# Batches 1 to 3 of a windowed attention: scores by quarters in shared bursts, value products as in batch 0, last stores by quadrant, and a new order

## The chip, the cores and the metric

The kernel runs on one core of a Trainium2 chip. The metric is the device time of one launch in microseconds, the median of several runs. One more execution was recorded by the profiler; all rows shown are from it.

## The reference, cut to what matters

```python
# q, k, v: (4 batches, 8 heads, 768 rows, 64), float32
scores = q @ k.T / 8
keep = (key < 4) | ((0 <= row - key) & (row - key < 128))     # 4 sink keys, a window of 128
a = softmax(where(keep, scores, -1e9))
x = (a @ v), heads side by side                               # (4, 768, 512)
h = relu(x.T @ w_tok1) @ w_tok2                               # mixes the 768 rows
u = x + h.T
out = u + relu(u @ w_ch1) @ w_ch2                             # mixes the 512 channels, 1536 hidden
```

## The kernel before

The work goes by *pairs* of heads: pair p is heads 2·(p mod 4) and the next of batch p div 4, so there are 16 pairs, 0 to 3 in batch 0. One pair's two heads lie on partitions 0 to 63 and 64 to 127, so that products with a contraction of 64 run two at a time on half of the array each (HALVES in the code), four at a time on a quarter each (QUARTERS) and eight at a time (EIGHTHS). Everything else uses the whole array (FULL). Scores are made with keys on partitions. A *group* g (0, 1, 2) of a pair is two blocks of 128 keys with the up to two blocks of 128 queries that see them; `scores(p, g)` writes it to one double bank of PSUM (there are two of these, tag `sc`), ScalarE takes the exponential into `pT`, and VectorE or GpSimd zeroes what lies outside the window. The four sink keys of two pairs are scored together by `score_sinks` (EIGHTHS). The value product multiplies `pT` and `pT_sink` with v, which has a column of ones beside it; VectorE takes the reciprocal of that column's result and scales into `x_sb`.

Batch 0 (`first_attention`) is scored on TensorE with its masks, and its value product is `pv(p, half)`: three query blocks of both heads, with one sink product on the whole array for both heads at a time. Pairs 4 to 15 are made by `attention_and_tokens`, with two bursts for each pair. The first burst holds group 0 in HALVES and the sink part of the value product of the pair before (`sink_values`, also HALVES, one head on each half of the array); `values(p, i)` then adds the window part of one head on the whole array. The second burst holds groups 1 and 2 in QUARTERS and, for even pairs, the sinks' scores:

```python
units.append(burst(scores(p, 0), sink_values(p - 1)))   # with transposed(p + 1) ahead for pairs 5 to 7
units += [values(p - 1, i) for i in range(2)]
units.append(burst(scores(p, 1), scores(p, 2), ...))    # turned_u and score_sinks where they are due
```

q and k arrive with rows on partitions. For pairs 0 to 3 SyncE loads them in float32 and engines cast them; for pairs 4 to 15 GpSimd's queue loads and casts them (two transfers for each of q and k, one for v), in the order written in `LOADS`, eight transfers at a time on the way: `q4` there is q of pair 4, `v` is v, `t` is w_tok, `c` a quarter of w_ch1, `d` a quarter of w_ch2. Pairs 4 to 7 are turned on TensorE (`turn`, `transposed`), pairs 8 to 15 by DMA transposes that SyncE issues (L500); the sinks' columns of kT are then copied to `kTs` by GpSimd or VectorE.

`mix_h` and `mix_u` are the mixing of rows (streams g and h for batch 0, k for the others). `mix_channels` is the mixing of channels: its first half (stream c) is plain for batch 0 and in seven half-size products in place of eight (Strassen's way, in Winograd's form) for batches 1 to 3; its second half, also by sevens, makes x (row blocks 0, 1, 3, 4) and y (2, 5). Each quadrant of a y or x result is added up on VectorE (L1223) into `o_sb`, and SyncE stores it (L1233).

TensorE's order is written out by hand in `ORDERED`, one word for each unit: `a17` is unit 17 of the stream of pairs 4 to 15, `c6` of the channels, and so on. The other engines' order is made by a planner (`Plan`) while the program is built, from written costs and the units' dependencies; at run time each engine takes its instructions in that fixed order and waits on semaphores. `done` maps names like `("qT", p)` to operations, on which others wait. Ahead of a unit stand also the PSUM banks that it needs (tag `mx`, four of them, beside the two double banks).

Of the kernel before, what the change touches and what calls it, by code (L numbers as in the profile page):

```python
# [17 lines left out]
def kernel(  # L18
# [72 lines left out]
    LATER = "cxyak"  # L91
# [380 lines left out]
    def prepare(p):  # L472
# [21 lines left out]
        free = ([("sk", p - 3)] if p >= 3 else [], [("s", p - NKB)] if p >= NKB else [])  # L494
# [109 lines left out]
    def scores(p, g):  # L604
# [4 lines left out]
        quarters = p >= NHP and g > 0  # L609
# [59 lines left out]
        if not by_pe:  # L669
# [8 lines left out]
            (190, 165, 140)[g] if quarters else width(g) * 0.47, run, deps, {} if by_pe else {"sc": [[x]]}, then,  # L678
# [30 lines left out]
    def pv(p, half):  # L709
# [36 lines left out]
        op = unit(460, run, deps, {"mx": [[r, n]]}, [r, n])  # L746
# [228 lines left out]
    def attention_and_tokens():  # L975

        tokens, units = [], []
        first, last = NHP, len(pairs) - 1
        prepare(first)
        units += [turn(first, n) for n in range(2)]  # L980
        for p in range(first, last + 1):
            b, hp = pairs[p]
            pieces = []
            if p < last:
                prepare(p + 1)
                if p + 1 < BY_DMA:
                    pieces.append(transposed(p + 1))
            pieces.append(scores(p, 0))
            if p > first:
                pieces.append(sink_values(p - 1))  # L990
            units.append(burst(*pieces))
            if p > first:
                units += [values(p - 1, i) for i in range(2)]
            pieces = [scores(p, 1), scores(p, 2)]
            if hp == 0 and p > first:
                tokens.append(mix_h(b - 1, 1, 0, NTOK))
                tokens += [mix_u(b - 1, 1, st, 2) for st in range(0, NT, 2)]
                if p <= BY_DMA:
                    pieces.append(turned_u(b - 1, 1))
            if hp == NHP - 1 and p < BY_DMA:  # L1000
                pieces.append(turned_u(b, 0))
            if hp % 2 == 0:
                pieces.append(score_sinks(p + 1))
            units.append(burst(*pieces))
            units[-1].then.append(sink_rows(p))
            if hp == 2:
                tokens.append(mix_h(b, 0, 0, NTOK))
                tokens += [mix_u(b, 0, st, 2) for st in range(0, NT, 2)]
        units += [pv(p, half) for half in range(2)]
        tokens.append(mix_h(b, 1, 0, NTOK))  # L1010
        tokens += [mix_u(b, 1, st, 2) for st in range(0, NT, 2)]
        return units, tokens

    def mix_channels(b):
# [196 lines left out]
        def products(t0, n):  # L1211
# [19 lines left out]
            def store(i):  # L1231
                def run(e):
                    in_order(nc.sync.dma_start(  # L1233
                        out=out[b, (QH * i + t0) * P:(QH * i + t0 + n) * P].rearrange("(t p) c -> p t c", p=P),
                        in_=tiles["o_sb", b, t0][:, i],
# [301 lines left out]
```

## Time and profile before

| | |
|---|---|
| median of three runs | 194.55 us (193.59 to 194.74) |
| profiled execution | 193.02 us, span from first to last instruction 191.3 us |
| TensorE busy | 181.8 us, 95% |
| VectorE, ScalarE, GpSimd busy | 163.7, 107.8, 89.2 us |
| moved by DMA | 26.31 MB, of it 11.80 MB in GpSimd's queue |
| granted TensorE clock | 0.998 of full speed |

In the profile's rows, PE is TensorE's products, PEld its weight loads, DVE is VectorE, ACT is ScalarE, POOL is GpSimd and SP is SyncE, with SPq its DMA issues. A timeline row is the start, the length, the engine, the line, the operation, output and inputs, the shape and how many alike were merged; in brackets stands the idle time ahead of it and what ended it. L157 is the line of the helper by which every matmul is recorded, so that rows are told apart by their tiles: `qT,kT` are scores, `v_sink,pT_sink` the sinks' value products, `v_aug,pT` the window's, `uT,w_ch` and `uT_sums,k_f` the first half of the channels, `w_ch,v1T`, `q_f,v1T` and `q_f,v_sums` the second.

### The profile page before, as it was taken

The page shows a single profiled execution, that of the slowest core. Times are in us where ns is not written, and L with a number is a line of the kernel's source. Part 1 is how long each engine was busy: PE and PEld are TensorE (multiplying, and loading weights), DVE is VectorE, ACT ScalarE, POOL GpSimd, SP SyncE. Part 2 cuts the span into 40 slices and gives each one's busy share as a digit, 9 for nine tenths or more (in the row PEclk, how much of TensorE's full clock was granted, in tenths as well). Part 3 has the DMA queues.
Part 4 walks back from the last instruction along what each step waited for, and adds up shares of the span by engine and source line. Part 5 has one row for each costly group of instructions (what it writes and reads, how often), then busy time and mean ns, then how long its engine had stood idle before and what let it go on. Part 6 is the DMA issues. An engine that isn't in the chain of part 4 may idle for free.

```text
span 191.3 us, 5397 instructions
## 1 busy us (share of the span) xinstructions
PE 181.8 (95%) x2170; PEld 132.5 (69%) x2173; DVE 163.7 (86%) x346; ACT 107.8 (56%) x199; POOL 89.2 (47%) x140
## 2 busy tenths in 40 slices
PE   6889889799999999999999999999999999999992
PEld 1336668466578787866657788876578887658882
DVE  4578848898999998889999999899899987789962
ACT  4499938687976724479785602676861103773000
POOL 7588879879499688453865350140160000000000
PEclk9999999999999999999999999999999999999999
DMA  6999999999999999999999999440102123500035
GB/s 185 251 288 180 178 166 191 186 170 207 173 147 171 113 116 154 181 175 232 186 132 149 137 115 137 167 174 0 33 0 55 29 48 130 211 0 0 0 113 219
DMA packets 92136, 26.31 MB, mean 137 GB/s; under 512 B 82384, under 2 KB 89040, under 8 KB 92112
## 3 DMA queue, kind: packets, MB, share of 16 engines
q0 software_dynamic: 67232, 11.80, 84.7%
q1 hardware_dynamic: 24880, 14.17, 36.5%
q8 instruction: 17, 0.28, 0.6%
q14 instruction: 7, 0.06, 0.1%
HBM read 26.75 MB, written 6.29 MB: 173 GB/s over the span
## 4 chain that ended last, share of the span: by engine, by line
PE 78%; DMA 16%; POOL 3%; issue 1%; SPq 1%; DVE 0%
PE ps L157 77%; DMA k_f<-in_k_dram 7%; DMA w_ch<-in_moe_w_ch_dram 5%; DMA v_aug<-in_v_dram 4%; POOL q_bf L142 1%; SPq L129 1%; POOL v_aug L150 1%; PE ps L542 0%; POOL w_ch L175 0%; POOL k_bf L166 0%; POOL w_tok L175 0%; PE ps L573 0%; DVE o_sb L1223 0%
## 5 line engine op out<-in xcount | busy, mean ns | idle before, releaser
L644 ACT ACTIVATE pT<-ps 128x1024 bf16<-128x1024 f32 (+1 forms) x48 | 44.2, 958 | 20.1 <-PE ps L157 19.8
L164 ACT ACTIVATE parts<-ps 128x384 f32<-128x384 f32 x51 | 23.2, 490 | 20.7 <-PE ps L157 19.3
L157 PE MATMUL ps<-uT,w_ch 128*128 128x384 bf16 x168 | 33.7, 326 | 0.6 <-DMA w_ch<-in_moe_w_ch_dram 0.6
L157 PEld LDWEIGHTS <-v1T 128*128 128x128 bf16 x288 | 28.0, 98 | 4.3
L1111 DVE CUSTOM_DVE_ANT_0 v1T<-ps,parts 128x384 bf16<-128x384 f32 x54 | 28.2, 548 | 2.7 <-PE ps L157 2.3
L157 PEld LDWEIGHTS <-w_ch 128*128 128x128 bf16 x204 | 19.0, 98 | 12.3 <-DMA w_ch<-in_moe_w_ch_dram 1.1
L170 ACT ACTIVATE v1T<-ps 128x384 bf16<-128x384 f32 x40 | 18.6, 498 | 10.2 <-PE ps L157 9.7
L157 PE MATMUL ps<-uT_sums,k_f 128*128 128x384 bf16 x108 | 23.4, 326 | 0.0
L157 PEld LDWEIGHTS <-v_sums 128*128 128x128 bf16 x216 | 20.5, 98 | 3.1 <-issue 0.5
L655 POOL TENSOR_SCALAR_AFFINE_SELECT pT<-pT 128x256 bf16<-128x256 bf16 (+1 forms) x28 | 14.1, 538 | 18.1 <-issue 16.5
L142 POOL DMA_DIRECT2D q_bf<-in_q_dram x24 | 19.7, 828 | 5.0 <-DMA q_bf<-in_q_dram 2.9
L142 POOL DMA_DIRECT2D k_bf<-in_k_dram x24 | 19.8, 835 | 3.3 <-DMA w_ch<-in_moe_w_ch_dram 1.4
L157 PEld LDWEIGHTS <-w_tok 128*128 128x128 bf16 x192 | 18.4, 98 | 4.0 <-issue 0.6
L157 PE MATMUL ps<-q_f,v1T 128*128 128x256 bf16 x144 | 19.5, 273 | 0.0
L1223 DVE TENSOR_TENSOR o_sb<-ps,u_sb 128x512 f32<-128x512 f32 (+1 forms) x32 | 17.0, 550 | 2.5 <-PE ps L157 2.2
L157 PE MATMUL ps<-w_ch,v1T 128*128 128x256 bf16 x144 | 19.2, 273 | 0.0
L157 PE MATMUL ps<-q_f,v_sums 128*128 128x256 bf16 x144 | 19.0, 273 | 0.0
L157 PEld LDWEIGHTS <-k_f 128*128 128x128 bf16 x144 | 13.5, 98 | 7.8 <-issue 0.6
L150 POOL DMA_DIRECT2D v_aug<-in_v_dram x16 | 16.6, 1036 | 4.2 <-DMA w_ch<-in_moe_w_ch_dram 1.7
L1223 DVE TENSOR_TENSOR o_sb<-ps,o_sb 128x512 f32<-128x512 f32 (+1 forms) x24 | 13.3, 556 | 4.7 <-PE ps L157 4.6
L157 PE MATMUL ps<-v_aug,pT 128*128 128x65 bf16 x352 | 16.0, 194 | 1.2 <-DMA v_aug<-in_v_dram 1.1
L157 PEld LDWEIGHTS <-pT 128*128 128x128 bf16 x352 | 14.1, 98 | 3.3 <-DMA v_aug<-in_v_dram 1.6
(89 smaller groups left out, 289.5 us busy)
## 6 DMA issues: line engine op xcount, KB each, us to landing
out_dram<-o_sb SPq DMA_DIRECT2D x8, 512.0 KB, 3.4
v_aug<-in_v_dram POOLq DMA_DIRECT2D x16, 192.0 KB, 9.6
w_ch<-in_moe_w_ch_dram POOLq DMA_DIRECT2D x8, 384.0 KB, 8.3
q_bf<-in_q_dram POOLq DMA_DIRECT2D x24, 96.0 KB, 9.3
k_bf<-in_k_dram POOLq DMA_DIRECT2D x24, 96.0 KB, 8.7
out_dram<-o_sb SPq DMA_DIRECT2D x8, 256.0 KB, 2.0
q_f<-in_q_dram SPq DMA_DIRECT2D x4, 384.0 KB, 6.0
k_f<-in_k_dram SPq DMA_DIRECT2D x4, 384.0 KB, 6.5
```

The lines of the kernel that those rows point to most:

```text
L129: in_order(nc.sync.dma_start(out=f, in_=rows_of(pidx, n).rearrange("p h j d -> p h (j d)")))
L142: in_order(nc.gpsimd.dma_start(out=out[:, h], in_=rows[:, h]))
L150: in_order(nc.gpsimd.dma_start(out=v_aug.rearrange("p i t d -> p (i t) d")[:, :, 0:D], in_=v[b].rearrange("h s d -> (h s) d")[2 * hp * S:2 ...
L157: in_order(nc.tensor.matmul(*args, skip_group_check=True, **kwargs))
L164: in_order(nc.scalar.activation(out, in_, AF.Copy))
L170: in_order(nc.scalar.activation(out, in_, AF.Relu))
L644: in_order(nc.scalar.activation(part(tiles["pT", p][:, :, ds(2 * g, 2)]), of_keys(tiles["ps_s", p, g])[:, :, 0:width(g)], AF.Exp, scale=scale,
L655: in_order(nc.gpsimd.affine_select(out=pt, in_=pt, compare_op=ALU.is_ge, fill=0.0, base=-n, pattern=[[0, nk], [1 - 2 * n, P]], channel_mul ...
L1111: in_order(nc.vector._custom_dve(TENSOR_ADD_SAT, out=v1_of(i, half), in0=ps, in1=kept[:, n], s0=HUGE, s1=0.0,))
L1223: in_order(nc.vector.tensor_tensor(out=sb(*out), in0=tiles["ps_out", b, t0, key[0]], in1=in1(), op=ALU.add,))
```

## The change

All scores of pairs 4 to 15 are now made in quarters. `attention_and_tokens` no longer makes two bursts for each pair: it lists the 36 groups (transposes ahead, the group, what goes with it, the copy of the sinks' rows) and puts two consecutive groups into one burst, pieces sorted by form; both double banks are then taken at once. So a burst holds groups 0 and 1 of an even pair, then its group 2 with group 0 of the odd pair and the sinks of both, then groups 1 and 2 of the odd pair. The value products become `pv(p, half)` as in batch 0, in a stream of their own (v), so that they can stand anywhere in the order. The stores of batch 3 go out by quadrants of 256 channels, each as soon as its last sum is made, in place of whole rows of 512. `ORDERED` and `LOADS` are written anew, and the planner's rule for when a DMA transpose may overwrite q names the scores as well as the sinks of the pair three before.

```diff
     ORDERED = (
-        "t0-1 m0-1 s0 t2 s1 m2 s2 t3 m3 s3 m4 o0 s4 t4 m5 t5 s5 o1-2 m6 s6 t6 m7 s7 t7 o3 m8 s8 o4 s9 a0 s10 m9 "
-        "s11 a1 m10 s12 o5 g0-1 o6-7 g2 o8 g3 a2 h0-1 g4 h2 g5 h3-4 g6 a3 g7 h5-7 c16 c10 a4-6 c6 c9 c7 c1 a7 "
...
-        "x52-53 x51 x45 x54-55 y26 y25 y22 y27"
+        "t0-1 m0-1 s0-1 t2 m2 t3 s2 m3 s3 o0 m4 s4 t4 m5 s5 o1 t5 o2 m6 s6 t6 m7 t7 s7 m8 a0 s8 o3-4 s9 m9 "
+        "s10-11 a1 m10 o5 s12 o6 g0 o7 g1 a2 o8 g2-4 h0 g5 h1 a3 h2 g6 h3-5 a4 v0 h6 g7 v1 c17 h7 c2 v2 c23 c1 "
+        "c0 a5 c18 v3 c22 c13 c8 c10 c12 a6 k0 c7 c9 c5 c14 c20-21 k1-3 c3 c19 v4 a7 x0-1 c11 v5 c6 c4 c16 c15 "
+        "v6-7 a8 x4-7 y0 x8-9 a9 x10-11 k4 y2 v8 k5 x12 y3 k6-7 x13 y4 v9 y5 a10 y1 y6 c24 c31 a11 x2 c33-34 x3 "
...
+        "c140 c144 x42 c149 c148 c142 x46 x43 y22 y21 x48 y23 x49 x47 x45 y24 x52-53 x50-51 y26 x54-55 y27 y25"
     )
     LOADS = (
-        "q4 v1 k4 t1 v2 t2 v3 q5 k5 k6 c1 v4 c3 c2 q6 c0 v5 q7 k7 d3 d1 d0 d2 q8 v6 k8 k9 v7 k11 q9 v8 q10 "
-        "v10 k10 k13 v9 q11 v11 k12 q12 k14 q13 v12 q14 q15 v13 k15 v15 v14 "
+        "k4 v3 q4 v1 q5 v2 t1 k5 t2 v4 k6 q6 k7 c3 c0 v5 q7 c1 d3 c2 d1 d0 d2 v6 q12 v7 q8 k8 k9 q9 v8 q10 "
+        "k10 k11 q11 v9 q14 v10 k12 k13 q13 v11 k14 v12 q15 k15 v13 v15 v14 "
     )
...
-        free = ([("sk", p - 3)] if p >= 3 else [], [("s", p - NKB)] if p >= NKB else [])
+        free = ([("sk", p - 3), ("s", p - 3)] if p >= 3 else [], [("s", p - NKB)] if p >= NKB else [])
...
-        quarters = p >= NHP and g > 0
+        quarters = p >= NHP
...
-                    nq = min(3, 2 * NT - a)
+                    nq = min(3 if a else 4, 2 * NT - a)
...
-        op = unit(460, run, deps, {"mx": [[r, n]]}, [r, n])
+        op = unit(540 if half else 365, run, deps, {"mx": [[r, n]]}, [r, n])
...
+            with_first, with_second = [], []
+            if p + 1 < min(BY_DMA, last + 1):
+                with_first.append(transposed(p + 1))
+            groups.append((with_first, scores(p, 0), [], sink_rows(p)))
+            if p % 2:
+                groups[-1][2].append(sinks.pop())
+            groups.append(([], scores(p, 1), with_second, None))
+            groups.append(([], scores(p, 2), [], None))
+            if p % 2 == 0:
+                sinks = [score_sinks(p + 1)]
...
+            out += [pv(p, half) for half in range(2)]
...
+        for n in range(0, len(groups), 2):
+            pieces = [x for k in range(3) for g in groups[n:n + 2] for x in (g[k] if k != 1 else [g[k]])]
+            pieces.sort(key=lambda x: x.form)
             units.append(burst(*pieces))
+            units[-1].then.extend(g[3] for g in groups[n:n + 2] if g[3] is not None)
...
+            if b < B - 1:
+                sent = {3: [store(0, deps=[a3, b2])], 5: [store(1, deps=[a5, c4])]}
+            else:
+                sent = {
+                    2: [store(0, 0, C2, [b2])], 3: [store(0, C2, C2, [a3])],
+                    4: [store(1, 0, C2, [c4])], 5: [store(1, C2, C2, [a5])],
+                }
```

The last TensorE units were x54-55, y26, y25, y22, y27; they are now y26, x54-55, y27, y25, so that the last store is one quadrant of one row block, 128 KB in place of 256 KB.

More of the change, by code (lines that the diff above doesn't have):

```diff
@@ L90 @@
     NSC, NMX = 2, 4
-    LATER = "cxyak"
+    LATER = "cxyakv"
     given = {}
@@ L677, in scores @@
         return piece(
-            (190, 165, 140)[g] if quarters else width(g) * 0.47, run, deps, {} if by_pe else {"sc": [[x]]}, then,
+            (195, 165, 140)[g] if quarters else width(g) * 0.47, run, deps, {} if by_pe else {"sc": [[x]]}, then,
             [("s", p)], form=QUARTERS if quarters else HALVES,
@@ L975, in attention_and_tokens, with tokens_of @@
     def attention_and_tokens():
-        tokens, units = [], []
+        tokens, units, out, groups = [], [], [], []
         first, last = NHP, len(pairs) - 1
+        def tokens_of(b, g):
+            tokens.append(mix_h(b, g, 0, NTOK))
+            tokens.extend(mix_u(b, g, st, 2) for st in range(0, NT, 2))
         prepare(first)
@@ L995, in attention_and_tokens @@
[L995 to L1005, printed above, removed]
@@ new lines, in attention_and_tokens @@
+            if p % 2:
[4 more added lines that the diff above has]
+                sinks = [score_sinks(p + 1)]
+            if hp == NHP - 1 and p < BY_DMA:
+                groups[-1][2].append(turned_u(b, 0))
+            out += [pv(p, half) for half in range(2)]
+            if hp == 1 and p > NHP + 1:
+                tokens_of(b - 1, 1)
+                if p <= BY_DMA + 1:
+                    with_second.append(turned_u(b - 1, 1))
@@ L1014, in mix_channels @@
+            if hp == 2:
+                tokens_of(b, 0)
+        tokens_of(pairs[last][0], 1)
+        for n in range(0, len(groups), 2):
+            pieces = [x for k in range(3) for g in groups[n:n + 2] for x in (g[k] if k != 1 else [g[k]])]
+            pieces.sort(key=lambda x: x.form)
+            units.append(burst(*pieces))
+            units[-1].then.extend(g[3] for g in groups[n:n + 2] if g[3] is not None)
+        return units, tokens, out
     def mix_channels(b):
@@ L1229, in evict, with store @@
                 return op
[L1231 removed]
+            def store(i, c0=0, cn=DM, deps=()):
                 def run(e):
                     in_order(nc.sync.dma_start(
[L1234 to L1235 removed]
+                        out=out[b, (QH * i + t0) * P:(QH * i + t0 + n) * P].rearrange("(t p) c -> p t c", p=P)[
+                            :, :, c0:c0 + cn],
+                        in_=tiles["o_sb", b, t0][:, i, :, c0:c0 + cn],
                     ))
[L1238 removed]
+                return Op({"SP": 380.0}, run, deps, traffic=n * STORE * cn / DM)
             a1 = evict("a1", (0, 0), lambda: u_block(0, 0))
```

29 lines of the change are left out of this document (5 added, 24 removed), and 19 rows, old and new, of the table ORDERED.

## The prediction

> **What bounds the kernel now.** I read the page first, then the chain that ended last, the busy time by stretches, and the timelines of single engines.
>
> ```profile
> PE 181.8 (95%) x2170; PEld 132.5 (69%) x2173; DVE 163.7 (86%) x346; ACT 107.8 (56%) x199; POOL 89.2 (47%) x140
> ...
> PE   6889889799999999999999999999999999999992
> ...
> PE 78%; DMA 16%; POOL 3%; issue 1%; SPq 1%; DVE 0%
> ```
>
> TensorE is busy in every slice after the first ten, and it makes 78% of the chain that ended last; the rest of the chain is the loads of the first 40 us and the last store:
>
> ```profile
> 30.13 9.18 DMA w_ch<-in_moe_w_ch_dram
> ...
> 73.08 114.82 PE ps L157 x1170
> ...
> 187.92 0.42 DVE o_sb L1223
> ```
>
> ```profile
> 0.00:8.00 8.00, 5.66 (x35) 2.00 (x35) 4.68 (x19) 3.71 (x7) 4.97 (x12) 1.00 0.84 212
> 8.00:20.00 12.00, 10.83 (x197) 6.48 (x198) 8.54 (x23) 10.76 (x17) 10.36 (x13) 1.00 1.72 231
> 20.00:42.00 22.00, 19.47 (x289) 13.97 (x286) 17.15 (x42) 15.72 (x32) 17.95 (x25) 1.00 1.91 178
> ...
> 42.00:187.70 145.70, 145.67 (x1655) 110.02 (x1654) 132.86 (x264) 77.59 (x145) 55.92 (x92) 1.00 1.11 118
> ```
>
> The second number after the colon is the length, the third TensorE's busy time. From 42 us on TensorE idles 0.03 us. So three things can move the end: TensorE's work itself, the time that it loses before 42 us, and the tail behind its last product. A new wait after 42 us would be a fourth.
>
> **A price list.** Busy times hold latency (a matmul shown with 326 ns lets the next one start after 163), so I price by starts: from the first matmul of one group to the first of the next.
>
> ```profile
> 63.39 0.82 PE L157 MATMUL ps<-q_f,v1T 128*128 128x256 bf16 x6
> 64.14 0.39 PE L157 MATMUL ps<-qT,kT 64*128 64x256 bf16 x4
> 64.37 0.29 PE L157 MATMUL ps<-v_sink,pT_sink 64*128 64x65 bf16 x8
> 64.59 0.84 PE L157 MATMUL ps<-v_aug,pT 128*128 128x65 bf16 x22
> ```
>
> ```profile
> 135.94 0.49 PE L157 MATMUL ps<-uT_sums,w_ch 128*128 128x384 bf16 x2
> 136.36 0.49 PE L157 MATMUL ps<-qT,kT 64*64 64x192 bf16 x16
> 136.78 0.50 PE L157 MATMUL ps<-uT,w_ch 128*128 128x384 bf16 x2
> ```
>
> ```profile
> 142.40 0.49 PE L157 MATMUL ps<-uT_sums,k_f 128*128 128x384 bf16 x2
> 142.72 0.35 PE L157 MATMUL ps<-v_aug,pT 128*128 128x65 bf16 x6
> ...
> 144.06 0.22 PE L157 MATMUL ps<-v_sink,pT_sink 128*128 128x130 bf16 x1
> 144.12 0.28 PE L157 MATMUL ps<-v_aug,pT 128*128 128x65 bf16 x4
> ```
>
> Two 128x384 take 0.32 (142.40 to 142.72), so 2.4 columns pass in a ns. The same two ahead of a burst take 0.42 (135.94 to 136.36): going into packed form costs 0.10. The sixteen quarter matmuls are, four at a time, 704 columns, 0.30; the next group starts after 0.42: the way back costs 0.12. Four half-array scores of group 0 take 0.23 (two at a time, 512 columns). The eight half-array sink products take 0.22, of which 0.11 is columns and 0.11 the way back. A sink product on the whole array takes 0.06.
>
> **The change, part by part.**
>
> *Fewer bursts.* Twelve pairs had two bursts each, 24; their 36 score groups two by two make 18. Six times 0.10 + 0.12 is -1.3 us.
>
> *Changes of form inside a burst.* Three bursts now go from halves (the transposes of pairs 5 to 7) to quarters, which the trace has nowhere: between 0 and the 0.12 of the way back; I take 0.10, +0.3. The Trainium skill (TensorEngine Tiling (Array Packing), Key Properties) says that a change of tiling mode, unlike a change of tile, drains TensorE. By it each of the three would pay like a way back, +0.36; by a free change 0.
>
> *Group 0 by quarters.* 256 and 192 columns instead of 512: 0.19 for 0.23, twelve times: -0.4.
>
> *Sink products on the whole array.* Four at 0.06 for eight halves worth 0.11: +0.13, for eleven pairs (the last one had it already): +1.4.
>
> Sum of TensorE's work: 0.0, bounds -0.4 and +0.4. VectorE, ScalarE and GpSimd keep their instructions almost to the piece (one mask moves from GpSimd to VectorE, 0.55 us, at an engine with 12.8 us to spare of the 145.7 above).
> *The order and the loads.* With these prices I added up the whole of TensorE's order: 175.8 us before, 175.9 after. A row's start minus the work ahead of it is what TensorE has lost by then.
>
> ```profile
> 18.60 0.23 PE L157 MATMUL ps<-v_sink,pT_sink 128*128 128x130 bf16 x1
> ...
> 25.42 0.36 PE L157 MATMUL ps<-v_aug,pT 128*128 128x65 bf16 x6 [0.76 <-DMA v_aug<-in_v_dram]
> ...
> 36.11 0.82 PE L157 MATMUL ps<-uT,w_ch 128*128 128x384 bf16 x4 [0.44 <-DMA w_ch<-in_moe_w_ch_dram]
> ...
> 42.06 0.49 PE L157 MATMUL ps<-qT,kT 64*64 64x192 bf16 x16
> ```
>
> Ahead of 18.60 stand 11.7 us of work (lost 6.9), ahead of 42.06 31.3 (10.8), ahead of 64.14 53.2 (11.0), and at the end 12.0 are lost. The first 6.9 hang on SyncE's loads of pairs 0 to 3, which do not change. The 3.9 up to 42.06 are waits like the two shown, for v and w_ch; the new order puts more batch 0 and 1 attention ahead of the first w_ch product (27.8 us of work instead of 26.2). What it pays for that comes earlier: k of pair 4 and v of pair 3 are now fetched ahead of q of pair 4 and v of pair 1.
>
> ```profile
> 10.10 1.63 POOL L142 DMA_DIRECT2D k_bf<-in_k_dram  x2
> ...
> 41.07 0.77 POOL L175 DMA_DIRECT2D w_ch<-in_moe_w_ch_dram  x1 [0.72 <-DMA v_aug<-in_v_dram]
> ...
> 45.27 1.67 POOL L142 DMA_DIRECT2D k_bf<-in_k_dram  x2
> ```
>
> ```profile
> k_bf<-in_k_dram POOLq DMA_DIRECT2D x1, 96.0 KB, 8.0
> ```
>
> ```profile
> w_ch<-in_moe_w_ch_dram POOLq DMA_DIRECT2D x1, 384.0 KB, 10.3
> ```
>
> ```profile
> k_bf<-in_k_dram POOLq DMA_DIRECT2D x1, 96.0 KB, 9.2
> ```
>
> The last column is issue to landing. The fourth load (k of pair 4, second half issued at 10.91) landed at 18.9; the last w_ch at 51.4; k of pair 8 (second half 46.08) at 55.3, and between these lie q8, v6 and k8: 1.3 us for each load. After, q of pair 4 is the fourth load, 18.9, and is wanted after 11.2 us of work, at 18.1: +0.8. v of pair 1 is the fifth, 20.2, wanted after 11.7, at 19.4 with that wait: +0.8, and w_tok1 +0.2. Lost by then: 8.7. Further on each load meets its first use within 1 us. VectorE's chain from the first u block (uT copies, w_ch sums, masks) has about 1.3 us more work than TensorE leaves room for between 24.6 and 28 us of work (before the same chain lay in the 3.9): +1.0, bounds 0 and 1.5. So 9.8 are lost ahead of the second half of batch 1, where before it was 10.8: **-1.0**, bounds -2.3 and +0.5.
>
> *The scores of pairs 8 and 9.* These are the first whose q and k are turned by SyncE's DMA transposes.
>
> ```profile
> 55.39 2.94 SPq L500 DMA_TRANSPOSE kT<-k_bf  x2
> ```
>
> ```profile
> 62.42 0.81 DVE L166 COPY kTs<-kT 64x4 bf16<-64x4 bf16 x2
> ```
>
> ```profile
> DMA to landing us min/median/max: 6.3/9.0/10.4
> ```
>
> Before, kT of pair 8 was asked for at 55.39 and used by the sink copy at 62.42, so it took at most 7.0; the last row is the six landings of kT that the trace shows. It can have been earlier: a load issued at 53.46 landed at 60.1. I take 5.5. TensorE wanted it at 64.14, so it was early. After, q12 and v7 are fetched ahead of k8, which lands two loads later, 57.9; kT at 63.4. TensorE, 1 us less behind, is there after 53.1 us of work, at 62.9: **+0.5** (at 7.0 after the issue +2.0, at 9.0 +4.0). Behind this burst the whole TensorE queue stands, and on GpSimd the copy of pair 8's sink columns waits for the same kT, with the loads of q11, v9 and all later ones behind it. Pair 9 comes up at 68.6 instead of 76.4; its q is two loads behind k8, so its transposes land between 67 and 70: I take **+0.1** (0 to 1.3). Later pairs have 3 us and more between landing and use by the same count, and later waits stay at the 1.0 of before.
>
> *Last stores by quadrant.*
>
> ```profile
> 188.37 0.34 SPq L1233 DMA_DIRECT2D out_dram<-o_sb  x1
> ```
>
> ```profile
> out_dram<-o_sb SPq DMA_DIRECT2D x8, 512.0 KB, 3.4
> ...
> out_dram<-o_sb SPq DMA_DIRECT2D x8, 256.0 KB, 2.0
> ```
>
> From this issue to the end (191.3) it is 2.9 us; the transfer is 256 KB. It becomes 128 KB, the other quadrant having left before. A store of 256 KB lands 1.4 us sooner than one of 512, so at most half of that, 0.7, is to be had from halving again; at least 0, if the fixed part rules. I take the middle, **-0.35**. The four stores more are issued on SyncE while products run.
>
> Sum: 0.0 - 1.0 + 0.5 + 0.1 - 0.35 = -0.75. The profiled execution took 193.02 us (span 191.3), so 192.3; the runs' median, 194.55, lies 1.5 above that execution, so 193.8 for a median.
>
> **Rivals.**
>
> *Transposes late (slower).* kT of pair 8 lands 7 to 9 us after its issue, at 64.9 to 66.9. TensorE waits 2.0 to 4.0 us instead of 0.5: 195.3 to 197.3, say 196.6. It decides from a landing later than 64.1 (no gain left). For it: the median of 9.0, and that transposes among loads are slow, while with no loads running they take
>
> ```profile
> uT<-u_sb SPq DMA_TRANSPOSE x3, 2.5
> ```
>
> 2.5 us. Against it: the 7.0 that this very transfer can have taken at most. The Trainium skill (DMA: Bandwidth & Descriptors, Issuing engines are not separate DMA queues) has DMAs of all issuers interleave on the same 16 engines; by it a transpose queues behind loads, as 9.0 against 2.5 shows.
>
> *The start loses less (faster).* The two early waits and VectorE's chain do not add but overlap: 7.5 to 8.3 lost at 35 us of work instead of 9.8, and the transposes' wait takes back no more than 0.5 of it: 192.0. For it: by the prices the w_ch waits of before are gone. Against it: the fourth landing, 18.9, does not depend on the order.
>
> *VectorE becomes the bound.*
>
> ```profile
> 73.00:93.00 20.00, 20.00 (x265) 14.80 (x256) 17.90 (x39) 14.09 (x25) 11.57 (x20) 1.00 1.69 187
> 93.00:113.00 20.00, 20.00 (x215) 14.85 (x212) 19.80 (x40) 11.76 (x23) 12.81 (x23) 1.00 2.06 142
> ```
>
> Its fifth number is VectorE: 17.9 and 19.8 of 20. A pair of heads now moved ahead brings some 3.4 us of masks and norms into the first stretch, which has 2.1 free: +1.3, so 195.1.
>
> *The packing alone decides.* The order brings nothing; work and tail stand: 194.2.
>
> **How the numbers follow.** Forecast 193.8 with 0.45; late transposes 0.18; a better start 0.20; VectorE 0.09; packing alone 0.08. Each stands for a spread of about 1 us. A measurement here tells about 1% (1.9 us) from no change: under 192.6 lie most of the better start and a little of the forecast's lower bounds, 0.24; over 196.5 more than half of the late transposes and some of VectorE, 0.15; within, 0.61. Range: 191.4 (start and tail at their good bounds) to 197.0 (transposes near the median).
>
> **What would show it.** Right: 18 bursts of quarters; TensorE waiting near 18 us for q of pair 4 and near 20 for v, hardly for w_ch; a gap of 0.5 us ahead of pair 8's quarters near 63; last store under 2.7 us from issue to end. Wrong: over 2 us lost at pair 8 or 9; TensorE under 99% busy between 70 and 187 us.

## The result, and the profile after the change

The changed kernel is slower: 197.15 us (median of 4, 196.46 to 197.26) against 194.25 (193.59 to 194.74), a ratio of 1.0131 with a 95% interval of 1.0088 to 1.0175. The forecast was 193.8, and 197.15 lies just above its range. The profiled execution took 197.21 us with a span of 195.5, 4.2 more than the span of before.

The timeline of TensorE shows one long gap (columns: start, busy time, engine and line, operation; in brackets the idle time ahead and what ended it):

```profile
63.69 0.28 PE L156 MATMUL ps<-v_aug,pT 128*128 128x65 bf16 x4
66.96 0.86 PE L156 MATMUL ps<-qT,kT 64*64 64x256 bf16 x16 [2.99 <-DMA kT<-k_bf]
67.75 2.74 PE L156 MATMUL ps<-q_f,v1T 128*128 128x256 bf16 x12
70.29 1.56 PE L156 MATMUL ps<-q_f,v_sums 128*128 128x256 bf16 x12
```

This is pair 8's first burst, waiting for pair 8's kT. The twelve products behind it start 2.54 us apart from the next twelve, where twelve of these take 1.3 elsewhere. The windows view says why (TensorE's clock is the third number from the end, 1 is full):

```profile
63.00:67.00 4.00, 1.01 (x31) 0.89 (x33) 3.79 (x9) 1.01 (x3) 0.19 (x2) 1.00 1.81 147
67.00:70.00 3.00, 3.00 (x27) 2.11 (x28) 0.00 (x0) 1.94 (x2) 2.28 (x6) 0.51 2.09 140
70.00:73.00 3.00, 3.00 (x28) 2.57 (x27) 2.47 (x5) 0.00 (x0) 2.89 (x4) 0.92 3.17 122
```

The granted clock is 0.51 from 67 to 70 us and 0.92 from 70 to 73: halved for some 3.4 us behind the gap, and half of that, 1.7 us, is lost (an estimate from these two windows). The Trainium skill (TensorE: Matmul & The Clock Gate, Part 1: The HAM clock gate) has a free-running window of 3.4 us, an idle one of which halves the clock; the length and the loss agree. The trigger does not: the gap here, 2.99 us, was shorter than such a window, and a later run shows 3.3 us of gap without a halved clock, so the traces don't settle what triggers it.

SyncE's queue and a row of the chain that ended last show how the transpose came to be late:

```profile
57.30 1.96 SPq L499 DMA_TRANSPOSE qT<-q_bf  x1
59.43 2.74 SPq L499 DMA_TRANSPOSE kT<-k_bf  x2
62.34 5.57 SPq L499 DMA_TRANSPOSE qT<-q_bf  x2
```

```profile
59.43 7.49 DMA kT<-k_bf
```

Pair 8's k had landed at 58.2, but SyncE was occupied with issuing qT until 59.3; kT was asked for at 59.43 and landed 7.49 us later, at 66.92.

The start has waits of its own, and the one for the cast of pair 3's k was not in the forecast:

```profile
17.54 0.35 PE L553 MATMUL ps<-ident,k_bf 64*128 64x64 bf16 x12 [0.87 <-POOL k_bf L165]
19.07 0.35 PE L553 MATMUL ps<-ident,q_bf 64*128 64x64 bf16 x12 [0.52 <-DMA q_bf<-in_q_dram]
20.47 0.36 PE L156 MATMUL ps<-v_aug,pT 128*128 128x65 bf16 x6 [0.89 <-DVE qT L165]
```

The profile puts the last wait down to VectorE's copy of qT, which ended at 20.45; v of pair 1 landed at 20.43, so that the row is counted as the wait for v below, though either would have held it. GpSimd's timeline of the changed kernel: the cast stands behind a load, whose issue waits 0.60 us for another load to land and takes 1.0. In the kernel before, the same cast started at 15.72.

```profile
15.64 1.01 POOL L149 DMA_DIRECT2D v_aug<-in_v_dram  x1 [0.60 <-DMA k_bf<-in_k_dram]
16.65 0.84 POOL L165 CAST k_bf<-k_f 128x768 bf16<-128x768 f32 x1
```

Taking the start of each product less the price of all work ahead of it, as the prediction does, TensorE of the changed kernel has lost 10.85 us at 50 us of work (before: 10.93), 3.06 more in the gap, 1.70 in the halved clock, and 0.34 in all that follows (before, after 50 us of work: 1.03). The priced work is 175.88 against 175.76, and the end is 0.1 longer. -0.1 + 3.1 + 1.7 - 0.7 + 0.1 + 0.1 = 4.2, the difference of the spans.

### The profile page after: what moved, and what is told of

Same layout as the page of the kernel before. It is cut to its first block, busy times and chain, and to the rows that moved or that the text cites. A ratio compares the mean times of both kernels' runs of the same rounds, so it can differ in the third digit from the quotient of the medians.

```text
span 195.5 us, 5417 instructions
## 1 busy us (share of the span) xinstructions
PE 182.1 (93%) x2177; PEld 133.6 (68%) x2177; DVE 166.4 (85%) x349; ACT 106.7 (55%) x197; POOL 88.3 (45%) x136
## 4 chain that ended last, share of the span: by engine, by line
PE 67%; DMA 24%; POOL 5%; issue 2%; ACT 1%; DVE 0%; POOLq 0%
PE ps L156 66%; DMA v_aug<-in_v_dram 11%; DMA k_bf<-in_k_dram 5%; DMA w_tok<-in_moe_w_tok_dram 4%; DMA kT<-k_bf 4%; POOL v_aug L149 1%; POOL w_ch L174 1%; POOL k_bf L141 1%; PE ps L541 0%; POOL v_sink L165 0%; POOL k_bf L165 0%; POOL w_tok L174 0%; POOL mask_add L209 0%; POOL mask_add L213 0%; ACT v_sink L163 0%
## 5 line engine op out<-in xcount | busy, mean ns | idle before, releaser
L163 ACT ACTIVATE parts<-ps 128x384 f32<-128x384 f32 x49 | 22.2, 493 | 22.7 <-PE ps L156 19.7
L156 PE MATMUL ps<-uT,w_ch 128*128 128x384 bf16 x168 | 34.2, 326 | 0.0
L654 POOL TENSOR_SCALAR_AFFINE_SELECT pT<-pT 128x256 bf16<-128x256 bf16 (+1 forms) x24 | 12.9, 569 | 18.0 <-issue 14.2
L156 PE MATMUL ps<-v_aug,pT 128*128 128x65 bf16 x352 | 18.4, 194 | 0.9 <-DVE qT L165 0.9
L156 PEld LDWEIGHTS <-pT 128*128 128x128 bf16 x352 | 16.7, 98 | 3.0 <-DMA v_aug<-in_v_dram 1.1
L156 PE MATMUL ps<-w_ch,v1T 128*128 128x256 bf16 x144 | 18.5, 273 | 0.0
L156 PE MATMUL ps<-q_f,v_sums 128*128 128x256 bf16 x144 | 18.4, 273 | 0.0
L732 DVE TENSOR_TENSOR x_sb<-ps,recip 128x384 bf16<-128x384 f32 x32 | 17.6, 552 | 0.8 <-DVE recip L729 0.2
## 6 DMA issues: line engine op xcount, KB each, us to landing
w_ch<-in_moe_w_ch_dram POOLq DMA_DIRECT2D x8, 384.0 KB, 10.3
```

The source lines that it names most:

```text
L156: in_order(nc.tensor.matmul(*args, skip_group_check=True, **kwargs))
L163: in_order(nc.scalar.activation(out, in_, AF.Copy))
L654: in_order(nc.gpsimd.affine_select(out=pt, in_=pt, compare_op=ALU.is_ge, fill=0.0, base=-n, pattern=[[0, nk], [1 - 2 * n, P]], channel_mul ...
L732: in_order(nc.vector.tensor_tensor(out=x_sb[b][:, ts(half, QH), ts(hp, 2 * D)].rearrange("p t (i d) -> p t i d", i=2), in0=tiles["ps_o", p ...
```

## The experiments

In all of them "lost" is counted as above. Times are medians; the kernel before was run beside each on the same chip (193.9 to 194.4).

**Pair 8's burst later.** One unit moved in the written order:

```
-"v6-7 a8 x4-7 y0 x8-9 a9
+"v6-7 x4-7 a8 y0 x8-9 a9
```

> The changed kernel with one unit moved: pair 8's first quarters come behind the four product units x4 to x7 instead of ahead of them. These are 24 products of 128x256 at 0.109 us (the row of 12 took 1.31 at full clock), 2.6 us. Late-transpose theory (T1: the loss is the one gap ahead of pair 8's quarters, and the halved clock that follows it): TensorE reaches those quarters near 66.5 us, kT of pair 8 lands near 66.9 as before, the gap is 0.5 us at most, the clock is granted in full behind it; 2.6 us of gap and 1.7 us of halved clock come back, 192.9 us for a median against 197.15. Order theory (R1: the new order as a whole makes TensorE wait for VectorE's and ScalarE's evictions, and the gap is only where that shows): the wait reappears behind the moved products, 196 us or more. Clock theory (R2: the halved clock belongs to that stretch of the program and not to the gap): the gap goes and the halved clock stays, 194.6 us.

Measured: 195.76 us (7 runs), ratio 1.0086 (1.0048 to 1.0124), span 193.5.

```profile
66.72 0.54 PE L156 MATMUL ps<-qT,kT 64*64 64x256 bf16 x16
71.86 0.38 PE L156 MATMUL ps<-qT,kT 64*64 64x256 bf16 x8 [2.27 <-DMA qT<-q_bf]
```

A row of its chain that ended last:

```profile
62.09 9.64 DMA qT<-q_bf
```

Pair 8 waits no more, but pair 9, whose q is turned next, does: 2.3 us, with the transpose 9.64 us under way. A third to a half of the loss comes back (the ratio falls from 1.0131 to 1.0086, the span by 2.0 of 4.2 us), not the 4.3 us expected. In the changed kernel this second wait was hidden behind the first. The clock stayed full in five of the seven executions, so the halved clock does not belong to the stretch: R2 is wrong.

**Pair 8's loads sooner.**

```
-d2 v6 q12 v7 q8 k8 k9 q9 v8 ... q11 v9 q14
+d2 v6 q8 k8 v7 k9 q9 v8 ... q11 v9 q12 q14
```

and x0 to x11 and y0 to y5 held to the small banks.

> The changed kernel with q and k of pair 8 fetched ahead of v of pair 7 and of q of pair 12 (which goes behind v of pair 9), and the products x0 to x11 and y0 to y5 held to the four small banks, so that the same order of TensorE can be planned. T1: k of pair 8 lands two loads, some 3 us, sooner (near 55 instead of 58.2), its transpose is asked for near 56 and lands between 61 and 64; the gap ahead of pair 8's quarters is 0 to 0.5 us, the clock stays full, 193 to 193.6 us. R1: 196 us or more. A third reading (R3: transposes wait for a lull in the loads, so that asking sooner does not help): kT of pair 8 lands at 66 or later all the same, and the time stays within 0.5 us of 197.15.

Measured: 197.97 us, ratio 1.0213 (1.0147 to 1.0279). TensorE, with pair 8's first burst in the first row, then SyncE and GpSimd:

```profile
65.76 0.46 PE L156 MATMUL ps<-qT,kT 64*64 64x256 bf16 x10
70.14 0.82 PE L156 MATMUL ps<-w_ch,v1T 128*128 128x256 bf16 x6 [0.69 <-DVE x_sb L733]
92.60 0.36 PE L156 MATMUL ps<-qT,kT 64*64 64x256 bf16 x7 [0.92 <-DVE x_sb L733]
```

```profile
56.81 3.47 SPq L500 DMA_TRANSPOSE kT<-k_bf  x2
```

```profile
65.77 1.96 POOL L165 COPY kTs<-kT 64x4 bf16<-64x4 bf16 x2 [3.95 <-DMA kT<-k_bf]
```

The gap at pair 8 is gone, but not as T1 has it: kT was asked for 2.6 us sooner and landed only 1.2 us sooner, at 65.76, 9.0 us after it was asked for. That is near the 66 of R3, which this run does not refute; the gap went also because TensorE itself came 1.7 us later (its last product ahead of the burst starts at 65.4, not 63.7). TensorE now waits for VectorE's x_sb and others in its place and loses 4.2 us after 50 us of work, so the time is not what T1 expected either. With the loads in another order, the planner had also put VectorE's instructions in another order; whether that or VectorE's load makes the waits was open.

**The gap filled with work.** 13 products of 128x512 that serve nothing ahead of pair 8's quarters:

```
+            if (p, g) == (2 * NHP, 0):
+                for _ in range(13):
+                    mm(tiles["ps_s", p, g][:, 0].rearrange("p k n q -> p (k n q)"), w_ch1[:, 0, 0:P],
+                       w_ch1[:, 0, 0:4 * P], start=True, stop=True)
```

> The changed kernel with 13 products of 128x512 that serve nothing (weights by weights, into the bank that pair 8's first quarters then overwrite) put ahead of these quarters: 13 times 0.219 is 2.8 us of work at full clock, just what TensorE waits there for kT of pair 8 (3.0 us). The transpose stays as late as it was. If the idle gap is what halves the clock (T1), the clock stays full and 1.7 us come back: 195.4 us, and the products behind the quarters run at 0.109 us each. If the halved clock belongs to the stretch or to the work in it (R2), nothing comes back: 197.1 us, more by up to 2.8 us if the gap did not last as long as the added work.

Measured: 196.58 us (195.47 to 197.84), the profiled execution 195.47, span 193.8. Timeline and windows of that execution:

```profile
64.16 2.75 PE L156 MATMUL ps<-w_ch 128*128 128x512 bf16 x12
66.84 0.55 PE L156 MATMUL ps<-qT,kT 64*64 64x256 bf16 x16
67.31 1.48 PE L156 MATMUL ps<-q_f,v1T 128*128 128x256 bf16 x12
```

```profile
67.00:70.00 3.00, 3.00 (x41) 2.58 (x34) 1.17 (x3) 1.94 (x2) 2.46 (x5) 1.00 2.04 127
```

```profile
66.09 0.66 POOL L165 COPY kTs<-kT 64x4 bf16<-64x4 bf16 x2 [2.77 <-DMA kT<-k_bf]
```

With the array busy the clock stays full, pair 8's burst starts 0.1 us from where it did, and the last matmul is 1.7 us earlier (189.98 against 191.72), as it should be without the halved clock. But the transpose landed at 66.09 here: an idle gap would have been some 2 us, and a gap of 2.3 us left the clock full in the first experiment. So it isn't shown that the added work kept the clock up. The times don't show it either: the median moved by 0.6 only, with a spread as wide as the effect, and the ratio is 1.016, not under 1.0131.

**Last stores by whole rows again.**

```
-            if b < B - 1:
+            if b < B:
                 sent = {3: [store(0, deps=[a3, b2])], 5: [store(1, deps=[a5, c4])]}
```

> The changed kernel with the last batch's stores by whole rows again, as before the change; all else as in the changed kernel. If storing by quadrant shortens the end (my term of -0.35), the time from the last matmul to the end of the span grows from 3.67 to about 4.0 us and the time by 0.35 us. If the end is set by the fixed part of a store and by what is issued behind one another on SyncE, it stays at 3.6 to 3.7 us, and the time within 0.2 us of 197.15.

Measured: 197.73 us (197.03 to 198.21). The last copy of VectorE in the changed kernel (span 195.5), in this one (195.3), and in the kernel before (191.3):

```profile
192.03 0.42 DVE L1225 TENSOR_TENSOR o_sb<-ps,o_sb 128x256 f32<-128x256 f32 x1 [0.23 <-PE ps L156]
```

```profile
190.90 0.42 DVE L1225 TENSOR_TENSOR o_sb<-ps,o_sb 128x256 f32<-128x256 f32 x1 [0.23 <-PE ps L156]
```

```profile
187.92 0.42 DVE L1223 TENSOR_TENSOR o_sb<-ps,u_sb 128x256 f32<-128x256 f32 x1 [0.23 <-PE ps L157]
```

From its start to the end of the span it is 3.5, 4.4 and 3.4 us. In the new order quadrants are worth 0.9 us, but with whole rows its end is 1.0 longer than that of the order before (why was not tried); each figure is from one execution. Together they give +0.1, where -0.35 was forecast. This execution also had a gap of 3.3 us at pair 8 and a clock of 1.00 behind it.

**Loads held back while pair 8 is turned.** The loads from v of pair 8 on wait on GpSimd for its copy of pair 8's sink columns (x0 to x11 and y0 to y5 are held to the small banks again):

```
+    done["kTs", 8].cost = {"POOL": 420.0}
+    done["v", 8].deps.append(("kTs", 8))
```

> The changed kernel, the order of TensorE untouched, with the loads of v of pair 8 and all behind it (q and k of pair 10 first) held on GpSimd behind its copy of pair 8's sink columns, which itself waits for kT of pair 8. So between 57 and 63 us no load is issued, and the transposes of pairs 8 and 9 run beside the few loads that are still under way (the last lands near 61). If a transpose is slow because loads share the DMA engines with it (T2: 7 to 10 us among loads, some 3 without), kT of pair 8, asked for near 59.5, lands between 62.5 and 64: the gap ahead of its quarters is 0 to 0.5 us instead of 3.0, and qT of pair 9 lands before 68. If the transposes are slow of themselves there (R3), kT of pair 8 lands at 66.5 or later with no load issued meanwhile and the gap stays. The time: pair 10's q and k come some 5 us later, near their use at 84 us; with no wait there 193.5 us, with one as long as the hold 197.

Measured: 197.58 us (10 runs), span 194.7. SyncE, GpSimd and TensorE:

```profile
59.83 2.60 SPq L500 DMA_TRANSPOSE kT<-k_bf  x2
```

```profile
62.64 0.46 POOL L165 COPY kTs<-kT 64x4 bf16<-64x4 bf16 x2 [5.63 <-DMA kT<-k_bf]
```

```profile
63.67 0.55 PE L156 MATMUL ps<-qT,kT 64*64 64x256 bf16 x16
67.95 0.82 PE L156 MATMUL ps<-w_ch,v1T 128*128 128x256 bf16 x6 [1.00 <-DVE x_sb L733]
83.66 0.54 PE L156 MATMUL ps<-qT,kT 64*64 64x256 bf16 x16 [1.03 <-DMA kT<-k_bf]
91.27 0.36 PE L156 MATMUL ps<-qT,kT 64*64 64x256 bf16 x7 [1.15 <-DVE x_sb L733]
```

T2 is shown: the same transpose, asked for 0.4 us later, takes 2.8 us with no loads issued beside it, against 7.5. The Trainium skill (DMA: Bandwidth & Descriptors, Issuing engines are not separate DMA queues) has the DMAs of all issuers share the engines; these two rows agree. The gap is gone (first row of TensorE), and again the time isn't gained: 4.6 us are lost after 50 us of work, to VectorE and to pair 10's transpose.

**Both bursts later, and the first loads and the cast.** Three kernels, each on top of the one before:

```
-"v6-7 a8 x4-7 y0 x8-9 a9 x10-11 k4 y2 v8 k5 x12
+"v6-7 x4-7 a8 y0 x8-11 k4 y2 a9 k5 x12 v8
```

> The changed kernel with both first bursts of quarters that use the transposes moved back: pair 8's behind x4 to x7 (as in the first experiment), the next one, which brings pair 9's, behind y0, x8 to x11, k4 and y2 (12 products of x, 12 of k4 and 6 of y2 more than there, 0.109 us each, 3.3 us). In the first experiment that burst stood at 69.3 us and its qT of pair 9 landed at 71.7; it now stands at 72.5. T1': both transposes are late by 2.3 to 3.1 us each, one hidden behind the other, and nothing else is wrong with the order from there on: no wait over 0.3 us after 50 us, what TensorE has lost stays at 11.4 to the end, the span is 191 to 191.5 us, the time equal to that of the kernel before within 0.5 us (193 to 194.4). R1 (VectorE, or a next transpose, takes the wait over again): 195 us or more, with a wait on x_sb or on kT of pair 10.

```
-k4 v3 q4 v1 q5
+q4 v1 k4 v3 q5
```

> As the experiment with both bursts later, and the first loads in another order: q of pair 4 and v of pair 1 ahead of k of pair 4 and v of pair 3 (q4 v1 k4 v3 instead of k4 v3 q4 v1). In the changed kernel TensorE waits 0.5 to 1.2 us near 19 us for q of pair 4 and 1.0 near 20.5 for v of pair 1. If these two waits are what the early order loses (S1), they go, nothing takes their place before 30 us, and the time is 1.0 to 1.5 us under that of the kernel with both bursts later, 192 to 192.5. If VectorE's and ScalarE's chain of copies behind them sets the pace anyway (S2: what is lost at 28 us is 10.3 to 11.4 whatever the two waits), TensorE waits as long for that chain between 20 and 30 us: the same time within 0.4 us.

```
-cost = {"POOL": 765.0} if p == NHP - 1 else
+cost = {"POOL": 765.0} if p == NHP - 1 and n == 0 else
```

> As the one before, and the cast of k of pair 3 on VectorE instead of GpSimd. In the changed kernel GpSimd first waits for a landing and issues a load (1.0 us) ahead of this cast, which starts at 16.65 instead of 15.72 before, and TensorE waits 0.9 us for it at 17.5. S1: this wait goes too, 0.6 to 0.9 us less than the kernel before it: 191.3 to 191.8 us, under the kernel before the change by over 1%. S2: the copies of VectorE, now with 0.56 us more, set the pace: the same time within 0.4 us, or 0.3 more.

Measured: 198.03, 198.93 and 199.62 us; all expectations of a gain failed. The first of them:

```profile
74.29 0.60 PE L156 MATMUL ps<-h1T,w_tok 128*128 128x256 bf16 x4 [1.32 <-ACT pT L643]
90.23 0.36 PE L156 MATMUL ps<-qT,kT 64*64 64x256 bf16 x7 [0.99 <-DVE x_sb L732]
```

No transpose is waited for, but ScalarE and VectorE are. With q of pair 4 and v of pair 1 first, their waits go, and others come in the same stretch, for two loads that moved back (the timeline of the third kernel; the second has both too, with 0.8 each):

```profile
23.47 0.36 PE L156 MATMUL ps<-v_aug,pT 128*128 128x65 bf16 x6 [1.11 <-DMA v_aug<-in_v_dram]
25.73 0.83 PE L156 MATMUL ps<-x_sb,w_tok 128*128 128x256 bf16 x6 [0.81 <-DMA w_tok<-in_moe_w_tok_dram]
```

At 30 us of work 11.5 us are lost, and 11.2 with the cast moved too (10.3 without either): what one load gains the next one loses. Neither S1 nor S2 as written.

**Is it the amount of VectorE's work?** In the loads-held, the changed and the earlier kernel most of the masking of pairs 8 to 13 is left out, so that a mask on VectorE takes 0.17 us instead of 0.55 to 0.7:

```
+            if 8 <= p <= 13:
+                pt, m = pt[:, :, 0:16], m[:, :, 0:16]
```

> As the experiment with the loads held behind pair 8's sink columns (no gap ahead of pair 8's quarters, but TensorE loses 4.6 us between 50 and 105 us all the same, most of it waiting for VectorE: 1.2 at 68 us and 1.4 at 91 for x_sb, 0.5 at 102), with the masks of pairs 8 to 13 on VectorE cut to 16 of their columns: this leaves out most of the masking of these pairs and takes 0.4 to 0.55 us off each of some 13 of VectorE's instructions between 60 and 110 us; the order on every engine stays. If VectorE's backlog is the second bound behind the gap (V1), the waits on x_sb go or shrink below 0.4 us each, the wait for kT of pair 10 at 83.7 (1.1) stays, and TensorE loses 1 to 2 us there instead of 4.6: a span of 191.5 to 192.5 against 194.7. If the waits come from the order in which VectorE and ScalarE stand, each waiting for TensorE or a transfer in its turn, and not from the amount of work (V2), 4 us or more stay lost, span 194 or more.

> The changed kernel with the same masks of pairs 8 to 13 cut to 16 of their columns (most of the masking of these pairs is left out), the orders untouched. If the late transpose alone makes the loss here (T1), nothing changes ahead of it: the gap at pair 8's quarters is 3.0 us again, with the halved clock behind it in some runs, and the time stays within 0.5 us of 197.2. If VectorE's backlog takes part in the loss (V1), 1 us or more comes back.

> The kernel before, with the masks of pairs 8 to 13 cut to 16 columns in the same way. TensorE loses 0.6 us there between 50 and 105 us, so at most that comes back: 193.5 to 194.2 (both theories). It is the control: if more than 1 us comes back, thinner masks help whatever the order, and the comparison above says nothing of the change.

Measured: 199.06, 197.04 and 194.43 us (the last: 0.9991, 0.9952 to 1.0031). In the first, the waits for x_sb stand as they did:

```profile
68.34 0.82 PE L156 MATMUL ps<-w_ch,v1T 128*128 128x256 bf16 x6 [0.87 <-DVE x_sb L735]
94.21 0.36 PE L156 MATMUL ps<-qT,kT 64*64 64x256 bf16 x7 [1.03 <-DVE x_sb L735]
```

In the second the gap at pair 8 is 3.1 us as ever. V1 is refuted for the masks' share of the work, and in the changed kernel itself less work on VectorE brings nothing back.

**Quadrants in the kernel before.** The store change alone.

> The kernel before with the last batch's stores by quadrants as in the changed kernel, and nothing else; every engine but SyncE has the same order. My term was -0.35 us (0 to -0.7). With whole rows in the changed order the end from the last matmul to the end of the span was 4.7 us, with quadrants 3.8; in the kernel before, with whole rows, 3.7. If what is in flight at the end sets the tail, quadrants bring 0.3 to 0.9 here too: 2.8 to 3.4 us. If the fixed part of the last store sets it, it stays at 3.6 to 3.7.

Measured: 194.33 us, 0.998 (0.9946 to 1.0015). The last copy starts at 189.28 of 192.6, 3.3 us from the end (3.4 with rows): no gain. That one small store sets the tail there would fit, but was not tried further. The wait that I took for pair 8's in this kernel (the third expectation of the next group speaks of it) is another; it stands in the middle of pair 7's value products, and the profile names no cause:

```profile
66.41 0.48 PE L157 MATMUL ps<-v_aug,pT 128*128 128x65 bf16 x10 [0.87 <-issue]
```

**The gap removed with every order in place.** A copy of one column of pair 8's kT on GpSimd, ahead of the first load issued after that transpose; in the changed kernel, in the first experiment's, and in the kernel before:

```
+    def hold():
+        for n, key in enumerate(((8, 1),)):
+            if key in asked and key not in held:
+                held.add(key)
+                in_order(nc.gpsimd.tensor_copy(out=scrap[:, n:n + 1], in_=asked[key][:, 0:1]))
```

> The changed kernel, the order of every engine as it is, with one instruction more: ahead of the load of q of pair 10 GpSimd copies one column of pair 8's kT to an unused tile, and so waits for that transpose; the loads of pair 10 are issued some 3 us later than in the changed kernel (v of pair 8 stays ahead). T2 (a transpose is late because loads run beside it): kT of pair 8 lands near 63 to 64.5 instead of 66.9, the gap shrinks from 3.0 to under 0.7 us and with it the halved clock. Then V2 (the waits of the earlier variants came from another order on VectorE and ScalarE): no wait for x_sb over 0.4 us follows, only one for kT of pair 10 near 83 us (0 to 1.5, since its loads are later); what is lost grows by 0.5 to 2 us between 50 us and the end instead of 5.1: span 191.5 to 193, time 193.3 to 195. V1' (without the gap VectorE is behind, whatever its order): x_sb is waited for again with 1 us or more at 68 and 91 us, and the span stays at 194.5 or more.

> The same one instruction, in the kernel of the first experiment (pair 8's first quarters behind x4 to x7), whose one wait was 2.3 us for qT of pair 9 at 71.9. T2: qT of pair 9 lands before 69.5, that wait goes. V2: no wait over 0.4 us on VectorE; 0 to 1.5 us for kT of pair 10: lost between 50 us and the end 0.3 to 2 us instead of 2.5, span 191 to 193. V1': VectorE waits of 1 us or more take its place, the span stays near 193.5.

> The same one instruction in the kernel before the change (ahead of the load of v of pair 8, where kT of pair 8 has been asked for; all orders as they are). In two of its three profiled executions TensorE waited 1.0 to 1.5 us near 66 us for pair 8's quarters, in one not at all. T2: that wait is gone in every execution: 0 to 1.2 us less, if the later loads have the room: 193.3 to 194.0 against 194.3. If the loads behind come too late for pairs 10 and on, 0.5 to 2 us more.

Measured: 196.96 us (ratio 1.0117, 1.0068 to 1.0166), 196.88 (1.0113, 1.006 to 1.0166) and 193.91 (0.9977, 0.9945 to 1.0009: no difference; the wait that its expectation speaks of was not pair 8's). The first:

```profile
64.64 0.54 PE L167 MATMUL ps<-qT,kT 64*64 64x256 bf16 x16 [0.15 <-DMA kT<-k_bf]
70.80 0.63 PE L167 MATMUL ps<-qT,kTs 64*32 64x512 bf16 x2 [0.48 <-POOL kTs L176]
72.85 0.63 PE L167 MATMUL ps<-qT,kTs 64*32 64x512 bf16 x2 [1.42 <-POOL kTs L176]
```

```profile
67.25 3.31 POOL L151 DMA_DIRECT2D k_bf<-in_k_dram  x4
70.50 0.49 POOL L176 COPY kTs<-kT 64x4 bf16<-64x4 bf16 x2
70.93 1.65 POOL L151 DMA_DIRECT2D q_bf<-in_q_dram  x2
72.62 0.42 POOL L176 COPY kTs<-kT 64x4 bf16<-64x4 bf16 x2
```

```profile
73.00:76.00 3.00, 3.00 (x15) 1.93 (x15) 0.00 (x0) 0.60 (x1) 3.00 (x5) 0.59 1.90 169
```

The gap is gone, no wait for x_sb comes, so the waits on VectorE in the earlier variants belonged to their other orders (V2). But the copies of the sink columns stand on GpSimd behind the issues of the postponed loads, TensorE waits for both, and the clock halves again. The second kernel has the same two waits, 0.6 and 1.4 us, instead of pair 9's. V1' is wrong, and so is the time that I expected from V2. These runs also show in the times what the halved clock costs: the two executions of the first kernel with a mean clock of 1.00 took 195.25 and 195.65 us, the four with 0.991 took 196.79 to 197.77; in the second it is 195.42 and 195.65 against 196.79 and more. In the kernel before, over all its runs here, a mean clock under 0.996 goes with 0.8 us only.

**And those copies on ScalarE.** On top of the added copy:

```
             def sinks_of(e):
+                e = "ACT" if p in (8, 9) else e
```

> The changed kernel with the one wait of GpSimd for pair 8's kT ahead of pair 10's loads, and the copies of the sink columns of pairs 8 and 9 on ScalarE instead of GpSimd; otherwise every engine's order as in the changed kernel. With the wait alone the gap ahead of pair 8's quarters was gone (0.15 us), VectorE was waited for nowhere, and TensorE instead waited 0.5 and 1.4 us at 70.8 and 72.9 for these two copies, which stood on GpSimd behind the postponed loads; the clock was halved behind that. Theory of the passed-on wait (P1: each mechanism is local, and the next one late is GpSimd's queue of loads): these two waits and the halved clock go, nothing over 0.5 us follows but kT of pair 10 (0 to 1.5 near 83): 0.4 to 2 us lost between 50 us and the end, span 191.5 to 193, time 193.2 to 194.8, as the kernel before or up to 0.5 us under it. Theory of a common bound (P2: the stretch from 55 to 75 us can't bring pairs 8 and 9 in time in this order, whichever queue is relieved): a wait of 1.5 us or more for a transfer shows in that stretch again, 196 us or more.

> The same, with pair 8's first quarters behind x4 to x7 as well (2.6 us later). P1: as above, and the wait for pair 8 is nil in every execution: span 191 to 192.5, time 193 to 194.3. P2: 195.5 us or more, with a wait for pair 9's q, or for copies that follow it.

Measured: 194.17 us (ratio 0.9984, 0.9953 to 1.0016, 12 runs) and 194.51 (1.0015, 0.9984 to 1.0046). Pair 8's first burst and the largest waits of the first kernel after 50 us, and a window of the stretch:

```profile
64.05 0.54 PE L167 MATMUL ps<-qT,kT 64*64 64x256 bf16 x16
82.40 0.38 PE L167 MATMUL ps<-qT,kT 64*64 64x256 bf16 x8 [0.56 <-ACT pT L656]
83.10 0.36 PE L167 MATMUL ps<-qT,kT 64*64 64x192 bf16 x8 [0.32 <-ACT pT L656]
```

```profile
72.00:75.00 3.00, 3.00 (x38) 2.73 (x36) 2.22 (x6) 0.60 (x1) 3.00 (x4) 1.00 2.44 121
```

One instruction added and the sink copies of two pairs, four small instructions, moved to another engine; in the trace TensorE and VectorE have the same instructions in the same order as in the changed kernel. The whole 1.3% is back, 3.0 us. P1 is right: the loss was the late transpose and what hung on it, and not a bound of the order. Neither version beats the kernel before.

## Why the prediction was wrong

*TensorE's work, 0.0:* right. By the same prices, hardly anything but 0.3 us is lost in the last 117 us of work.

*The start, -1.0* (its parts add up to 9.7 us lost, not 9.8): it came to -0.1 at 50 us of work. The waits, counted by starts, for q of pair 4 (0.8 forecast, 0.6 measured), v of pair 1 (0.8; 1.0) and VectorE's chain (1.0; 1.3) were near. Missing was pair 3's cast behind a load's issue on GpSimd (+0.9), and late copies of v's sink rows on ScalarE that hold up an eviction at 54 us (+0.4). I counted what the order moves on TensorE and the DMAs, and not what a moved load stands ahead of on GpSimd.

*Pair 8, +0.5:* this is the step that failed. It was 3.06. kT landed at 66.92 instead of 63.4: 0.3 us because k landed at 58.2 and not at 57.9, 1.2 because kT was asked for at 59.43 and not at that landing, as SyncE needed 1.96 us for qT's issue, and 2.0 because it took 7.5 instead of 5.5. The 5.5 lay under every row shown for kT (6.3 the least, 9.0 the median; for this transfer only a bound, 7.0 at most). The loads beside the transpose are the larger part: asked for sooner, at 57.96 (the kernel with both bursts later) and at 56.81 (that with pair 8's loads sooner), it still landed at 66.3 and 65.8. The alternatives stood beside it, +2.0 at 7.0, and so did the mechanism as a rival: late transposes, 195.3 to 197.3, with a chance of 0.18.

*What the gap does to the clock* was in no term: 1.7 us in the profile.

*Pair 9, +0.1:* not tested by the changed kernel, where it stood behind pair 8's gap; alone it is 2.3 us (first experiment), above the bound of 1.3.

*The tail, -0.35:* +0.1. By one execution each, quadrants did more than forecast, 0.9, and the new order's end, which I had not costed, took it away; in the kernel before they bring nothing.

*Later waits as before, 1.0:* 0.34, better.

*The median 1.5 above the sum:* true of the kernel before, whose profiled execution (193.02) was a quick one; the changed kernel's (197.21) was at its median. So 4.2 us between the spans are 2.9 between the medians.

*The rivals:* late transposes is what happened, with 197.15 inside its span of times. That the time fits so well is in part luck: its price has neither the halved clock (1.7) nor the start and the tail that failed to bring their 1.35. VectorE as the bound is refuted in this kernel. The packing alone (194.2) is where the kernel stands once the late transpose and its copies are out of the way (194.17): a better start did not come.

## What to carry to other kernels

A transfer that runs beside a stream of loads should be costed at the durations seen among loads, and its issue at the time its queue is free; if one value decides the sign, take the row and not the hope under it. When work is moved ahead, check each queue that feeds it (the transposes' issuer, the loads ahead of them, the small copies behind the loads): here the two transposes and the copies each kept TensorE waiting for 2 to 3 us, and curing one only showed the next. Asking sooner for a transfer that stands among loads gained less than half of the time by which it was asked sooner; keeping loads out of its way took it from 7.5 to 2.8 us. To see whether a gap is the cause, remove it with all orders in place: variants that let a planner choose anew lost the gain elsewhere and nearly hid the cause.

## What was not expected of the hardware

The same DMA transpose took 2.8 us with no load issued meanwhile (in the loads-held kernel, and again in the same with thin masks), 5.7 with one load of 192 KB just ahead of it (asked for at 58.93, used at 64.64), and 7.5 among loads. In the nine traces with loads issued beside it, it landed 6.4 to 9.0 us after it was asked for, but always 2.8 to 4.2 us after GpSimd had issued the last load ahead of its own wait for kT. Whether a transpose shares the DMA engines with the loads or waits until they run out is not told apart by these runs. Mean clocks come in steps: of the changed kernel's four executions three had 0.991 and one 0.982, and 0.009 of 195 us is 1.7, one halved stretch. A step doesn't always show in the time: the execution at 0.982 was the quickest of the four. Gaps of 3.0 and 3.1 us were followed by one, gaps of 2.3 and 3.3 us in other profiled executions were not, and two shorter waits close together (0.5 and 1.4) were; what decides it stays open.
